# A hand-fixed order for all engines, with attention values one unit late and the causal mask on GpSimd, in a fused attention and gated-MLP kernel

## The chip, the cores and the metric

The kernel runs on one core of one Trainium2 chip. The metric is the device time of one execution in microseconds (us). Engines are named as in the profile: PE (TensorE), PEld (TensorE's weight loads), DVE (VectorE), ACT (ScalarE), POOL (GpSimd), SP (the queue that issues most DMAs).

Two states occur. Most runs of the kernel before took 436 to 441 us; one took 717.93 us, and that one was the profiled one. All comparisons below use fast runs.

## The reference, cut to what matters

The input x is 2048 x 640. It is layer-normalised, and two branches share the result. The product of both is added to x.

```python
xn = layernorm(x)                                   # 2048 x 640
# branch A: 32 heads of 20 columns, 4 segments of 512 rows
for s in range(4):
    logits = q[s] @ k[s].T * scale + causal_mask
    a_dot  = softmax(logits) @ v[s]
    a_mem  = (phi(q[s]) @ M) / (phi(q[s]) @ z + 1e-6)   # phi(t) = t+1 if t>0 else exp(t)
    o      = g * a_mem + (1 - g) * a_dot
    M += phi(k[s]).T @ v[s];  z += phi(k[s]).sum()
# branch B: sigmoid(xn @ w_gate) * (xn @ w_up) @ w_down, widths 640 -> 1536 -> 640
return x + (o @ wo) * silu(B(xn))
```

## The kernel before

Per segment there are eight groups of four heads. The scores of a group come in three units, so that the lower triangle alone is computed. Each unit's scores fill one accumulator tile `Sps` of four banks (four heads, one 32-row tile of the TensorE array each). ScalarE takes the exponential, VectorE multiplies the diagonal blocks by a mask, and TensorE then multiplies with V. All of this is in one unit, in the program's order:

```python
UNITS = [[(0, 0, 512, 0)], [(1, 0, 384, 128), (3, 384, 128, 384)], [(2, 0, 256, 256)]]
def attn_group(n, g, st_):
    for ui, unit in enumerate(UNITS):
        with prio(C0):
            for r in range(4):
                for (kb, c0, ncol, q0) in unit:
                    nc.tensor.matmul(Sps[:, r, c0:c0 + ncol], ..., tile_position=(32 * r, 0))
        nc.scalar.activation(pt[:], Sps[:, :, 0:ntot], ACT.Exp, scale=SCALE)
        for (kb, c0, ncol, q0) in unit:
            nc.vector.tensor_tensor(pt[:, :, c0:c0 + P], ..., cmask..., op=ALU.mult)
        ... # 8 or 16 matmuls of 21 columns each into Aps, then its eviction
```

Wk and Wq are loaded into a temporary tile and reordered by ScalarE (`nc.scalar.copy`, four times). The gate and up weights are loaded again for each segment. The order of the instructions of each engine is found by the framework's scheduler from priorities. Three accumulator banks, `ps_d`, serve everything but the attention.

Of the kernel before, what the change touches and what calls it, by code (L numbers as in the profile page):

```python
# [7 lines left out]
P = 128  # L9
S = 2048  # L10
D = 640
H = 32
DH = 20
NSEG = 4
# [4 lines left out]
TT = S // P  # L19
NG = 8  # L20
EPS = 1e-5
SCALE = DH ** (-0.5)

# [4 lines left out]
AX = mybir.AxisListType  # L28
PSUM = bass.MemoryType.PSUM

PAIRS = [(0, 0), (1, 0), (2, 0), (2, 1), (3, 1), (4, 1)]
PAIRS_OF_BANK = {0: [0, 1, 2], 1: [3, 4, 5]}
# [3 lines left out]
def kernel(  # L36
# [13 lines left out]
    dbg: bass.AP = None,  # L50
):
    nc = tc.nc

    PRIO_STRIDE = 1_000_000
    C0, CA, CB, CC = 0, 1, 2, 3
    prio_cnt = {}

    class prio:
        def __init__(self, cls):
            self.cls = cls  # L60

        def __enter__(self):
            self.saved = tc.cur_priority
            tc.cur_priority = self.cls * PRIO_STRIDE + prio_cnt.get(self.cls, 0)

        def __exit__(self, *a):
            prio_cnt[self.cls] = tc.cur_priority - self.cls * PRIO_STRIDE
            tc.cur_priority = self.saved
            return False

# [8 lines left out]
    stg = ctx.enter_context(tc.tile_pool(name="stg", bufs=2))  # L79
# [4 lines left out]
    wpool = ctx.enter_context(tc.tile_pool(name="wpool", bufs=2))  # L84
    xpool = ctx.enter_context(tc.tile_pool(name="xpool", bufs=2))

    dpool = ctx.enter_context(tc.tile_pool(name="dscratch", bufs=1, space=bass.MemoryType.DRAM))
    Qs = [dpool.tile([2 * 336, L], BF, name=f"Qs{i}") for i in range(2)]
    Ks = [dpool.tile([D, L], BF, name=f"Ks{i}") for i in range(2)]

    ident = cpool.tile([P, P], BF, name="ident")
    nc.gpsimd.memset(ident[:], 0.0)
    nc.gpsimd.affine_select(out=ident[:], in_=ident[:], compare_op=ALU.not_equal, fill=1.0,
                            base=0, pattern=[[-1, P]], channel_multiplier=1)

    cmask = cpool.tile([P, P], BF, name="cmask")
    nc.gpsimd.memset(cmask[:], 1.0)
    nc.gpsimd.affine_select(out=cmask[:], in_=cmask[:], compare_op=ALU.is_ge, fill=0.0,
                            base=0, pattern=[[1, P]], channel_multiplier=-1)
# [5 lines left out]
    Wd = cpool.tile([P, FC, D], BF, name="Wd")  # L105


    with prio(CC):
        beta_b = cpool.tile([P, H], BF, name="beta_b")
        nc.sync.dma_start(beta_b[:], A_beta.partition_broadcast(P))  # L110
        th = cpool.tile([P, H], F32, name="th")
        nc.scalar.activation(th[:], beta_b[:], ACT.Tanh, scale=0.5)
        gcol = cpool.tile([P, H], F32, name="gcol")
        omg = cpool.tile([P, H], F32, name="omg")
        ginv = cpool.tile([P, H], F32, name="ginv")
        nc.vector.tensor_scalar(gcol[:], th[:], 0.5, 0.5, op0=ALU.mult, op1=ALU.add)
        nc.vector.tensor_scalar(omg[:], th[:], -0.5, 0.5, op0=ALU.mult, op1=ALU.add)
        nc.vector.reciprocal(ginv[:], gcol[:])
        ginv_s = cpool.tile([P, H], F32, name="ginv_s")
        nc.vector.tensor_copy(ginv_s[:].rearrange("p (a r g) -> p a r g", a=2, r=4),  # L120
                              ginv[:].rearrange("p (a g r) -> p a r g", a=2, g=4))

        epst = cpool.tile([P, 1], F32, name="epst")
        nc.vector.memset(epst[:], EPS)

        B16 = cpool.tile([P, 16], F32, name="B16")
        nc.gpsimd.memset(B16[:], 0.0)
        for t in range(8):
            nc.gpsimd.affine_select(out=B16[:], in_=B16[:], compare_op=ALU.not_equal, fill=1.0,
                                    base=-16 * t, pattern=[[-1, 16]], channel_multiplier=1)  # L130
        Ind = cpool.tile([P, DC, H], F32, name="Ind")
        nc.gpsimd.memset(Ind[:], 0.0)
        for c in range(DC):
            if c < 2:
                nc.gpsimd.tensor_copy(Ind[:, c, 0:16], B16[:])
            elif c > 2:
                nc.gpsimd.tensor_copy(Ind[:, c, 16:32], B16[:])
            else:
                nc.gpsimd.tensor_copy(Ind[0:64, c, 0:16], B16[0:64, :])
                nc.gpsimd.tensor_copy(Ind[64:128, c, 16:32], B16[64:128, :])  # L140

        BD = cpool.tile([P, len(PAIRS), 16, DH + 1], BF, name="BD")
        nc.gpsimd.memset(BD[:], 0.0)
        for pi, (c, b) in enumerate(PAIRS):
            if c != 2:
                nc.gpsimd.tensor_copy(BD[:, pi], B16[:].unsqueeze(2).to_broadcast([P, 16, DH + 1]))
            else:
                lo, hi = (0, 64) if b == 0 else (64, 128)
                nc.gpsimd.tensor_copy(BD[lo:hi, pi], B16[lo:hi, :].unsqueeze(2).to_broadcast([hi - lo, 16, DH + 1]))

        Mbd = cpool.tile([P, len(PAIRS), 16 * (DH + 1)], BF, name="Mbd")

        QTp = cpool.tile([P, NG, L], BF, name="QTp")
        KTp = cpool.tile([P, NG, L], BF, name="KTp")
        nc.gpsimd.memset(QTp[:], 0.0)
        nc.gpsimd.memset(KTp[:], 1.0)


    Sps = ps_s.tile([P, 4, L], F32, name="Sps")

    xnT_of = {}

    def layernorm_chunk(n):
        xnT = xpool.tile([P, DC, L], BF, name="xnT")
        xnT_of[n] = xnT
        xt4 = lnp.tile([P, 4, D], BF, name="xt4")
        nc.sync.dma_start(xt4[:], x2[n * L:(n + 1) * L, :].rearrange("(j p) d -> p j d", p=P))
        mv4 = lnp.tile([P, 4, 2], F32, name="mv4")
        for j in range(4):
            st = lnp.tile([P, 2, 6], F32, name="st")  # L170
            nc.vector.bn_stats(st[:, 0, :], xt4[:, j, 0:D // 2])
            nc.vector.bn_stats(st[:, 1, :], xt4[:, j, D // 2:D])
            nc.vector.bn_aggr(mv4[:, j, :], st[:])
        sd4 = lnp.tile([P, 4], F32, name="sd4")
        nc.scalar.activation(sd4[:], mv4[:, :, 1], ACT.Sqrt, bias=epst[:], scale=1.0)
        rstd4 = lnp.tile([P, 4], F32, name="rstd4")
        nc.vector.reciprocal(rstd4[:], sd4[:])
        for j in range(4):
            xn = lnp.tile([P, D], BF, name="xn")
            nc.vector.tensor_scalar(xn[:], xt4[:, j, :], mv4[:, j, 0:1], rstd4[:, j:j + 1],  # L180
                                    op0=ALU.subtract, op1=ALU.mult)
            pT = ps_d.tile([P, DC, P], BF, name="pT", tag="d")
            for c in range(DC):
                nc.tensor.transpose(pT[:, c, :], xn[:, c * P:(c + 1) * P], ident[:])  # L184
            nc.vector.tensor_copy(xnT[:, :, j * P:(j + 1) * P], pT[:])

    seg_state = {}

    def phi_from(src, dst_pool, name, bufs):
        mn = stg.tile([P, L], BF, name="mn")  # L190
        nc.vector.tensor_scalar(mn[:], src, 0.0, None, op0=ALU.min)
        ex = stg.tile([P, L], BF, name="ex")
        nc.scalar.activation(ex[:], mn[:], ACT.Exp)
        ph = dst_pool.tile([P, L], BF, name=name, bufs=bufs)
        nc.vector.scalar_tensor_tensor(out=ph[:], in0=src, scalar=0.0, in1=ex[:], op0=ALU.max, op1=ALU.add)  # L195
        return ph

    def qkv_K(n, c, st_):
        T0 = n * L
        ps = ps_d.tile([P, L], F32, name="psk", tag="d")  # L200
        for k in range(DC):
            nc.tensor.matmul(ps[:], lhsT=Wk[:, k, c * P:(c + 1) * P], rhs=xnT_of[n][:, k, :],  # L202
                             start=(k == 0), stop=(k == DC - 1))
        if c == 0:
            st_["ktd5"] = stg.tile([P, DC, L], BF, name="ktd5", bufs=1)
        ktd = st_["ktd5"][:, c, :]
        nc.vector.tensor_copy(ktd, ps[:])
        if c == DC - 1:
            nc.sync.dma_start(Ks[n % 2].rearrange("(c p) n -> p c n", p=P), st_["ktd5"][:])
        nc.vector.tensor_reduce(out=st_["kabs"][:, c:c + 1], in_=ktd, axis=AX.X, op=ALU.max,  # L210
                                apply_absolute_value=True)
        nc.vector.tensor_scalar(st_["IK"][:, c, :], Ind[:, c, :], st_["kabs"][:, c:c + 1], -1.0,
                                op0=ALU.mult, op1=ALU.mult)
        if n < NSEG - 1:
            st_["phiKT"].append(phi_from(ktd, stg, "phikt", 5))
# [233 lines left out]
    with prio(CB):  # L449
# [11 lines left out]
        for s_ in qkv_steps(0):  # L461
            s_()
# [69 lines left out]
```

## Time and profile before

The median of four runs was 437.36 us (436.31 to 717.93). The page of the profiled run, which fell in the slow state, begins so. A line has busy us, the share of the span, and the number of instructions of each engine.

```profile
span 716.2 us, 8687 instructions
PE 670.2 (94%) x3530; PEld 282.3 (39%) x3560; DVE 284.2 (40%) x711; ACT 268.8 (38%) x290; POOL 18.2 (3%) x49
```

Read alone it says "TensorE-bound". The timeline of TensorE, below, says why that is not to be carried over to the 437 us runs. Columns are start, length, engine, line, operation, operands, count.

```profile
653.84 2.61 PE L339 MATMUL up<-xnT,wu 128*128 128x512 bf16 x5
656.17 2.61 PE L335 MATMUL gp<-xnT,wg 128*128 128x512 bf16 x5
658.50 2.61 PE L339 MATMUL up<-xnT,wu 128*128 128x512 bf16 x5
```

Groups of five matmuls of 512 columns start 2.33 us apart, 466 ns for each matmul. (The lengths shown, 2.61 us, overlap, because the profile models a matmul's end.) The Trainium skill, "TensorE: Matmul & The Clock Gate", Part 1, gives 215.7 ns for this shape on a warm array.

The groups that the argument is about, from part 5 of the same page (busy us, mean ns of one, then the idle time before them):

```profile
L388 ACT ACTIVATE pt<-Sps 128x2048 bf16<-128x2048 f32 (+1 forms) x96 | 152.9, 1593 | 136.9 <-PE Sps L383 123.9
L390 DVE TENSOR_TENSOR pt<-pt,cmask 128x512 bf16<-128x512 bf16 x128 | 51.2, 421 | 78.4 <-ACT pt L388 78.2
L383 PE MATMUL Sps<-QTp,KTp 21*128 21x128 bf16 (+3 forms) x512 | 46.7, 394 | 15.1 <-ACT pt L388 14.3
```

### The profile page before, as it was taken

The numbers are of one execution on the slowest core, as the hardware profiler recorded it, in microseconds if no ns is written. First come the engines' busy times: TensorE is split into PE (matmuls) and PEld (weight loads), VectorE is DVE, ScalarE is ACT, GpSimd is POOL, SyncE is SP. The second block draws the span as 40 slices with busy tenths as digits, with TensorE's granted clock in tenths as the row PEclk, the third lists the DMA queues.
The fourth block names the chain that finished last, engine by engine and source line by source line (L and its number), as shares of the span: only waits on it lengthen the run. The fifth ranks groups of instructions, "written<-read, shape, count | busy, mean of one in ns | idle before, by whom it ended". The sixth has DMA issues, their size and how long they took to land.

```text
span 716.2 us, 8687 instructions
## 1 busy us (share of the span) xinstructions
PE 670.2 (94%) x3530; PEld 282.3 (39%) x3560; DVE 284.2 (40%) x711; ACT 268.8 (38%) x290; POOL 18.2 (3%) x49
## 2 busy tenths in 40 slices
PE   2799999999999999996999999999699999999997
PEld 1235333334355543332335544333233554333454
DVE  4754566423323676411223457342112344511122
ACT  4632458555413543325413552022541355311111
POOL 9000000000000000000000000000000000000000
DMA  9623022112201001223120010031412001121010
GB/s 305 190 72 97 3 91 78 49 33 83 59 18 38 6 15 39 81 66 76 38 74 19 19 38 1 18 100 43 99 38 73 20 19 38 38 68 42 1 37 19
DMA packets 51432, 40.16 MB, mean 56 GB/s; under 512 B 2592, under 2 KB 50080, under 8 KB 51392
## 3 DMA queue, kind: packets, MB, share of 16 engines
q1 hardware_dynamic: 51392, 39.60, 18.9%
q8 instruction: 28, 0.46, 0.3%
q14 instruction: 12, 0.10, 0.0%
HBM read 31.60 MB, written 8.00 MB: 55 GB/s over the span
## 4 chain that ended last, share of the span: by engine, by line
PE 90%; ACT 4%; issue 3%; DVE 2%; POOL 0%; another core or an unknown queue 0%; ACTq 0%; POOLq 0%
PE yp L429 15%; PE up L339 14%; PE gp L335 14%; PE psv L257 6%; PE sp L439 6%; PE psk L202 6%; PE Sps L383 6%; PE psq L221 6%; PE Aps L396 5%; ACT pt L388 3%; PE dm L284 3%; PE am L362 3%; PE po L420 1%; PE cps L243 1%; PE pT L184 1%
## 5 line engine op out<-in xcount | busy, mean ns | idle before, releaser
L388 ACT ACTIVATE pt<-Sps 128x2048 bf16<-128x2048 f32 (+1 forms) x96 | 152.9, 1593 | 136.9 <-PE Sps L383 123.9
L339 PE MATMUL up<-xnT,wu 128*128 128x512 bf16 x229 | 121.8, 666 | 2.3 <-issue 1.6
L335 PE MATMUL gp<-xnT,wg 128*128 128x512 bf16 x229 | 120.2, 666 | 3.0 <-issue 2.5
L429 PE MATMUL yp<-Wd,hT 128*128 128x320 bf16 x384 | 117.2, 498 | 0.0
L390 DVE TENSOR_TENSOR pt<-pt,cmask 128x512 bf16<-128x512 bf16 x128 | 51.2, 421 | 78.4 <-ACT pt L388 78.2
L344 DVE SCALAR_TENSOR_TENSOR hT<-tg,up 128x512 bf16<-128x512 bf16 x48 | 32.9, 686 | 116.5 <-PE up L339 111.4
L342 ACT ACTIVATE tg<-gp 128x512 bf16<-128x512 f32 x48 | 28.5, 597 | 127.5 <-PE gp L335 125.6
L429 PEld LDWEIGHTS <-hT 128*128 128x128 bf16 x384 | 53.3, 144 | 44.0 <-issue 13.0
L383 PE MATMUL Sps<-QTp,KTp 21*128 21x128 bf16 (+3 forms) x512 | 46.7, 394 | 15.1 <-ACT pt L388 14.3
L396 PEld LDWEIGHTS <-pt 128*128 128x128 bf16 x1280 | 47.2, 102 | 30.6 <-issue 16.5
L335 PEld LDWEIGHTS <-wg 128*128 128x128 bf16 x240 | 32.9, 141 | 62.2 <-issue 60.7
L339 PEld LDWEIGHTS <-wu 128*128 128x128 bf16 x240 | 32.6, 138 | 61.5 <-issue 59.5
L396 PE MATMUL Aps<-vaug,pt 128*128 128x21 bf16 x1280 | 53.4, 178 | 0.9 <-DVE phikt L195 0.3
L221 PE MATMUL psq<-xnT,Wq 128*128 128x512 bf16 x97 | 48.0, 666 | 4.9 <-ACT Wq L457 4.0
L439 PE MATMUL sp<-Wo,oT 128*128 128x320 bf16 x160 | 51.1, 497 | 0.0
L257 PE MATMUL psv<-Wv,xnT 128*128 128x320 bf16 x160 | 49.8, 489 | 0.0
L202 PE MATMUL psk<-xnT,Wk 128*128 128x512 bf16 x95 | 47.0, 666 | 1.8 <-issue 1.2
L383 PEld LDWEIGHTS <-KTp 21*128 21x128 bf16 x512 | 11.5, 91 | 77.7 <-issue 75.8
L433 DVE SCALAR_TENSOR_TENSOR aa<-t,yp 128x320 bf16<-128x320 bf16 x32 | 15.6, 486 | 59.9 <-ACT t L432 59.9
L432 ACT ACTIVATE t<-yp 128x320 bf16<-128x320 f32 x32 | 14.0, 436 | 56.5 <-PE yp L429 56.5
L257 PEld LDWEIGHTS <-xnT 128*128 128x128 bf16 x160 | 20.5, 134 | 25.9 <-issue 15.3
L439 PEld LDWEIGHTS <-oT 128*128 128x128 bf16 x160 | 22.5, 145 | 18.9 <-issue 6.2
(82 smaller groups left out, 468.7 us busy)
## 6 DMA issues: line engine op xcount, KB each, us to landing
wg<-in_B_w_gate_dram SPq DMA_DIRECT2D x24, 320.0 KB
wu<-in_B_w_up_dram SPq DMA_DIRECT2D x24, 320.0 KB
QTp<-Qs SPq DMA_DIRECT2D x32, 84.0 KB
xt<-in_A_x_dram SPq DMA_DIRECT2D x4, 640.0 KB
Ks<-ktd SPq DMA_DIRECT2D x4, 640.0 KB
KTp<-Ks SPq DMA_DIRECT2D x32, 80.0 KB
xr<-in_A_x_dram SPq DMA_DIRECT2D x16, 160.0 KB
out_dram<-xr SPq DMA_DIRECT2D x16, 160.0 KB
```

The source lines that it names most:

```text
L202: nc.tensor.matmul(ps[:], lhsT=Wk[:, k, c * P:(c + 1) * P], rhs=xnT_of[n][:, k, :], start=(k == 0), stop=(k == DC - 1))
L221: nc.tensor.matmul(ps[:], lhsT=Wq[:, k, c * P:(c + 1) * P], rhs=xnT_of[n][:, k, :], start=(k == 0), stop=(k == DC - 1))
L257: nc.tensor.matmul(ps[:], lhsT=xnT_of[n][:, k, j * P:(j + 1) * P], rhs=Wv[:, k, half * (D // 2):(half + 1) * (D // 2)], start=(k == 0), st ...
L335: nc.tensor.matmul(gp[:], lhsT=wt["g"][:, k, fo:fo + P], rhs=xnT_of[n][:, k, :], start=(k == 0), stop=(k == DC - 1))
L339: nc.tensor.matmul(up[:], lhsT=wt["u"][:, k, fo:fo + P], rhs=xnT_of[n][:, k, :], start=(k == 0), stop=(k == DC - 1))
L344: nc.vector.scalar_tensor_tensor(out=h[:], in0=tg[:], scalar=1.0, in1=up[:], op0=ALU.add, op1=ALU.mult)
L383: nc.tensor.matmul(Sps[:, r, c0:c0 + ncol], lhsT=KTp[32 * r:32 * r + DH + 1, g, kb * P:(kb + 1) * P], rhs=QTp[32 * r:32 * r + DH + 1, g, q ...
L388: nc.scalar.activation(pt[:], Sps[:, :, 0:ntot], ACT.Exp, scale=SCALE)
L390: nc.vector.tensor_tensor(pt[:, :, c0:c0 + P], pt[:, :, c0:c0 + P], cmask[:].unsqueeze(1).to_broadcast([P, 4, P]), op=ALU.mult)
L396: nc.tensor.matmul(Aps[:, qb, r, :], lhsT=pt[:, r, off:off + P], rhs=st_["V"][kb][:, 16 * (g // 4) + 4 * r + (g % 4), :], start=first, sto ...
L429: nc.tensor.matmul(yp[:], lhsT=hT[f][:, j * P:(j + 1) * P], rhs=Wd[:, f, hs], start=(f == 0), stop=(f == FC - 1))
L439: nc.tensor.matmul(sp[:], lhsT=oT[:, c, :], rhs=Wo[:, c, hs], start=(c == 0), stop=(c == DC - 1))
```

## The change

Its intent is to leave nothing to the scheduler. Every engine's order is the program's order. A list of "A" work (next segment's normalisation, projections, memory) and a queue of "B" work (gate, up, down, output) are dealt out so that each of the 96 score units gets the same amount of TensorE work beside it. The attention values of a unit are computed one unit later, in the middle of that filler. In detail:

- the mask becomes a GpSimd `affine_select`;
- gate and up weights stay in SBUF; Wk and Wq are used in the order in which they lie in memory, and the DMA that lays K and Q out sorts the heads;
- the memory's matrices shrink from 6 blocks of 336 columns to 5 blocks of 147 or 168, block-diagonal by head;
- |q| is taken by VectorE as a bit mask, 1/sqrt by GpSimd as a power; ScalarE keeps only functions of one table;
- 14 warm-up matmuls stand at the start.

The core of the diff, cut:

```diff
-            nc.scalar.activation(pt[:], Sps[:, :, 0:ntot], ACT.Exp, scale=SCALE)
-            for (kb, c0, ncol, q0) in unit:
-                nc.vector.tensor_tensor(pt[:, :, c0:c0 + P], pt[:, :, c0:c0 + P],
-                                        cmask[:].unsqueeze(1).to_broadcast([P, 4, P]), op=ALU.mult)
+        nc.scalar.activation(pt[:, :, 0:ntot], Sps[:, :, 0:ntot], ACT.Exp, scale=SCALE)
+        for (kb, c0, ncol, q0) in unit:
+            nc.gpsimd.affine_select(out=pt[:, :, c0:c0 + P], in_=pt[:, :, c0:c0 + P], compare_op=ALU.is_ge,
+                                    fill=0.0, base=0, pattern=[[0, 4], [1, P]], channel_multiplier=-1)
 ... (cut)
         for g in range(NG):
-            with prio(CA):
-                attn_group(n, g, st_)
-            with prio(CB):
-                for s_ in step_slices[g]:
-                    s_()
 ... (cut)
+            for ui in range(NU):
+                slot = g * NU + ui
+                scores(g, UNITS[ui])
+                pt = exps(ui, UNITS[ui])
+                due += rate
+                pop(slot, due - rate / 2)      # half of this unit's filler
+                if pend is not None:
+                    attend(*pend)              # attention values of the unit before
+                pend = (n, g, ui, pt)
+                pop(slot, due)                 # the other half
```

## The prediction

> **What bounds the kernel now.** The profiled execution is not the one to beat: it took 717.93 us, the three other runs 436.3 to 438.3. In the trace TensorE is busy 94% of 716 us. The chain of waits has five back-to-back 128x512 matmuls in 2.33 us, 466 ns each, although the granted clock reads 1.000; VectorE and ScalarE durations look ordinary. The Trainium skill ("TensorE: Matmul & The Clock Gate", Part 1) gives 426.7 ns cold and 215.7 ns warm at N=512; 466 is near the cold one. I take the 436 us runs to be warm; this trace cannot show that.
>
> TensorE's warm load, estimated from the program's columns: projections, GLU, memory, transposes 660,000 columns / 2.4 = 275 us, plus about 5 us fixed cost; scores 1.36 us per group of heads in the trace, halved, x32 = 21 us; the 1280 attention-value matmuls, 27 ns each in bursts (the timeline), 35 us at either clock. Sum 335 us. So the fast run idles TensorE about 100 us: it is no longer bound by TensorE but by start-up and handoffs. Start-up: ScalarE reorders Wk and Wq (4 x 3.15 us, with 1.28 us table loads), Q is not begun before 29.5 us and the first score is at 61 us (slow clock; I estimate 47 warm). Handoffs: one score buffer, exponentials of 1.88 us, 1.88 us and 1.02 us per group, ScalarE 269 us and VectorE 284 us in all, and matmuls queued in program order.
>
> **What changes.** Removed: the weight reordering (12.6 us ScalarE), the Sqrt tables, and Abs (12.5 us on ScalarE, now on VectorE); the mask product on VectorE (51.2 us), which goes to GpSimd, where a 512-element select costs an estimated 0.55 us, 70 us in all, hidden because attention values are taken one unit later; gate and up weights loaded once, not four times (DMA is idle, worth little); memory matmuls narrowed from 48,000 to 18,000 columns (12.6 us warm). Added: cheap warm-up matmuls, and a fixed order which gives every score unit about 2.5 us of filler on TensorE, half before and half after the previous unit's attention values. Since exponential plus handoff takes about 2.2 us, the next scores should usually find their buffer free. ScalarE and VectorE work of the body falls only little: about 2.5 us and 2.6 us per unit against TensorE's 3.1.
>
> **On the critical path.** Warm TensorE load after: 335 - 12 = 323 us. Start-up: scores should begin at about 31 us, since the K and Q spills stand behind 7 MB of loads (305 GB/s in the first slice before); TensorE has some 20 us of work by then, so about 12 us are lost. Tail: 4 us. That is 339 us without a stall. In the body, in-order engines at 80% load and three shared accumulators should cost 5 to 8% of 300 us, 18 us.
>
> **Prediction: 357 us, range 341 to 380. Faster by over 2%: 0.97; within 2%: 0.02; slower: 0.01.** If the profiled execution is again slow, its span should still be 650 to 700 us, because there TensorE's load rules: the gain shows only at the warm clock.
>
> **What would show each step.** 128x512 matmuls at about 216 ns apart in a warm trace; TensorE idle under 40 us; first score near 31 us; ScalarE total 235 to 250 us; mask groups on GpSimd near 0.55 us; memory groups a third of the columns; waits of scores on exponentials small.
>
> **What would make it wrong.** GpSimd selects slowed by sharing SBUF access with VectorE, so attention values wait; phi exponentials (up to 1536 columns) ahead of a score exponential; loads delaying the spills beyond 35 us; or the clock falling in gaps.

## The result, and the profile after

The changed kernel took 387.97 us (median of 11 runs, 386.88 to 390.41), all fast. The kernel before took 438.33 us (median of its 16 runs, the four above among them). The ratio of the fast runs is 0.8858 (95% interval 0.8831 to 0.8885). Ratios here are the mean time of one kernel's fast runs over that of the other's of the same rounds, so not quite the ratio of the medians. The change is 11% faster, but 31 us slower than predicted, and above the upper end of the range.

To compare like with like I ran the kernel before again, unchanged, for a profile. Its page (span, part 1, the granted clock in 40 slices, and the chain that ended last) reads:

```profile
span 436.1 us, 8717 instructions
PE 379.9 (87%) x3560; PEld 204.4 (47%) x3560; DVE 275.1 (63%) x711; ACT 265.0 (61%) x290; POOL 18.4 (4%) x49
PEclk9968999989999999999969999899977999999999
PE 65%; DVE 17%; ACT 12%; issue 3%; DMA 1%; POOL 1%; SPq 0%; ACTq 0%; DVEq 0%; POOLq 0%
```

The same lines of the changed kernel, and its groups for the mask, the exponentials and the attention values:

```profile
span 386.5 us, 8606 instructions
PE 355.4 (92%) x3522; PEld 199.5 (52%) x3566; DVE 234.3 (61%) x526; ACT 232.9 (60%) x247; POOL 101.2 (26%) x169
PEclk9899999999999998999999998999999999999989
PE 68%; DVE 15%; ACT 8%; issue 4%; DMA 4%; POOL 0%; SPq 0%; DVEq 0%; ACTq 0%
L427 ACT ACTIVATE pt<-Sps 128x2048 bf16<-128x2048 f32 (+1 forms) x96 | 152.8, 1592 | 59.6 <-PE Sps L419 56.9
L429 POOL TENSOR_SCALAR_AFFINE_SELECT pt<-pt 128x512 bf16<-128x512 bf16 x128 | 84.2, 668 | 262.7 <-ACT pt L427 262.7
L443 PE MATMUL Aps<-V,pt 128*128 128x21 bf16 x1280 | 46.9, 173 | 0.3 <-POOL pt L429 0.3
```

Two things are to be read. The mask costs GpSimd 84 us, and GpSimd waits 262.7 us for exponentials, yet TensorE waited 0.3 us for the mask. And TensorE is shown busy for 355.4 of 386.5 us, 31 us idle, which would fit the prediction's "under 40 us". That figure deceives: a matmul is shown busy for longer than its share of the array, so gaps of 0.1 us between two matmuls vanish in it.

A better account counts starts. In the fast traces the matmuls' starts, back to back, are 216 ns apart at 512 columns, 136 at 320, 56 at 128, and 25.5 for the attention values' 21 columns. The program's matmuls at these distances, without the scores, come to 301 us in the changed kernel (its 14 warm-up matmuls not counted) and 312 us in the one before. The scores' columns come to 17 us in both, if the four row tiles run together. What is left of each span is neither. (I computed this from the starts in the trace; the few 512-column records that are missing from it are counted.)

| us | before | after | predicted for after |
|---|---|---|---|
| matmuls without scores, at full pace | 312 | 301 | 302 |
| scores, columns alone | 17 | 17 | 21 in all |
| switches into and out of score blocks (see below) | about 20 | 20 | 0 |
| lost before the first score | 29 | 13 | 12 |
| lost in the body (waits, half clock) | 54 | 24.5 | 18 |
| lost after the last attention values | 4 | 11 | 4 |
| span | 436 | 386.5 | 357 |

The switches' row is 96 times 0.21 us, which an experiment below measured; the lost time of the body is what then remains. The device time lies about 1.5 us over the span. So the change gained 11 us of TensorE work, 16 us of start-up and about 29 us in the body, and it gave 7 us back at the end. Against the prediction, 16 us went to the scores, 7 us to the end, 6.5 us to the body and 1 us to the start.

Part of the body's loss is the clock. By the clock events of the two traces TensorE had half its clock for 27 us of the body before and for 7 us of it after. At half pace that is at most 14 and 3 us of the 54 and 24.5 us.

What TensorE waited for in the kernel before, in the fast state (total us, times, longest):

```profile
PE Sps L383 <- ACT pt L388: 18.5, 14, 3.7
PE pT L184 <- POOL B L129: 12.3, 1, 12.3
PE psq L221 <- ACT Wq L457: 8.0, 2, 5.4
PE Aps L396 <- DVE pt L390: 4.9, 13, 0.9
```

The second is the wait before the first matmul of all, the third the wait for Wq, which ScalarE reorders: both belong to the start. The same view of the changed kernel, with the line that corresponds to the first of these last:

```profile
PE pk L306 <- DVE ktd L301: 5.2, 3, 2.6
PE pT L205 <- DVE xn L191: 3.4, 5, 1.2
PE po L393 <- DVE odot L387: 1.9, 1, 1.9
PE Sps L419 <- ACT pt L427: 1.1, 3, 0.4
```

Scores hardly wait for exponentials any more (1.1 us against 18.5). Waits at the segment boundaries are new at the top: `pk` is the transposition of phi(K), once per boundary.

The trace shows three places to look at. First, a block of scores in the timeline (the PEld row is its weight load):

```profile
329.63 0.84 PE L407 MATMUL sp<-Wo,oT 128*128 128x320 bf16 x5
330.40 0.10 PEld L419 LDWEIGHTS <-KT 21*128 21x128 bf16 x4 [0.26 <-issue]
330.40 0.40 PE L419 MATMUL Sps<-QT,KT 21*128 21x512 bf16 x4
330.73 1.04 PE L353 MATMUL gp<-xnT,Wg 128*128 128x512 bf16 x4
```

Five matmuls of 320 columns should take 0.68 us at 136 ns; the block starts 0.77 us after them. The block's four matmuls run side by side, 512 columns, 0.214 us; the next matmul starts 0.33 us later. So about 0.09 us is lost ahead of the block and 0.12 us after it. The weights of the small tile are loaded only at 330.40, when the large matmuls are through.

Second, a segment boundary:

```profile
142.82 0.34 PE L306 MATMUL pk<-ident,ktd 128*128 128x128 bf16 x3
143.16 0.88 DVE L182 BATCH_NORM_STATS2 st<-xt 128x6 f32<-128x320 bf16 x2
144.20 0.64 DVE L301 TENSOR_TENSOR ktd<-ktd,mn 128x1024 bf16<-128x1024 bf16 x1
144.89 0.84 PE L306 MATMUL pk<-ident,ktd 128*128 128x128 bf16 x12 [1.72 <-DVE ktd L301]
```

TensorE needs the last piece of phi(K), the addition at 144.20. In front of it in VectorE's queue stands a statistic of the next segment's normalisation, which nobody needs soon. TensorE waits 1.72 us, and soon after the granted clock is halved for 3.4 us (the 8 in the 16th slice of the clock row).

Third, the end, where the last residual rows are loaded into a buffer that is still being stored:

```profile
377.99 0.33 SPq L399 DMA_DIRECT2D xr<-in_A_x_dram  x1
380.31 0.49 DVE L413 TENSOR_TENSOR xr<-aa,xr 128x640 bf16<-128x640 bf16 x1 [1.39 <-DMA xr<-in_A_x_dram]
380.70 0.33 SPq L399 DMA_DIRECT2D xr<-in_A_x_dram  x1
383.04 0.49 DVE L413 TENSOR_TENSOR xr<-aa,xr 128x640 bf16<-128x640 bf16 x1 [1.44 <-issue]
```

### The profile page after: what moved, and what is told of

It is laid out like the page before. It is cut to its first block, busy times and chain, and to the rows that moved or that the text cites. A ratio compares the mean times of both kernels' runs of the same rounds, so it can differ in the third digit from the quotient of the medians.

```text
span 386.5 us, 8606 instructions
## 1 busy us (share of the span) xinstructions
PE 355.4 (92%) x3522; PEld 199.5 (52%) x3566; DVE 234.3 (61%) x526; ACT 232.9 (60%) x247; POOL 101.2 (26%) x169
## 4 chain that ended last, share of the span: by engine, by line
PE 68%; DVE 15%; ACT 8%; issue 4%; DMA 4%; POOL 0%; SPq 0%; DVEq 0%; ACTq 0%
PE psq L222 11%; PE yp L376 11%; PE up L362 10%; PE gp L353 10%; PE Aps L443 6%; PE Sps L419 5%; ACT pt L427 4%; PE sp L407 4%; PE psv L280 4%; DVE hT L365 3%; DVE st L182 2%; DMA xt<-in_A_x_dram 2%; PE cps L266 1%; PE pk L306 1%; ACT mn L295 1%
## 5 line engine op out<-in xcount | busy, mean ns | idle before, releaser
L429 POOL TENSOR_SCALAR_AFFINE_SELECT pt<-pt 128x512 bf16<-128x512 bf16 x128 | 84.2, 668 | 262.7 <-ACT pt L427 262.7
L362 PE MATMUL up<-xnT,Wu 128*128 128x512 bf16 x224 | 59.8, 383 | 1.5 <-DVE omem L346 0.4
L353 PE MATMUL gp<-xnT,Wg 128*128 128x512 bf16 x223 | 58.1, 379 | 2.9 <-ACT oT L395 1.7
L376 PE MATMUL yp<-Wd,hT 128*128 128x320 bf16 x384 | 57.5, 299 | 0.1
L443 PE MATMUL Aps<-V,pt 128*128 128x21 bf16 x1280 | 46.9, 173 | 0.3 <-POOL pt L429 0.3
L419 PE MATMUL Sps<-QT,KT 21*128 21x128 bf16 (+3 forms) x512 | 35.6, 303 | 2.3 <-ACT pt L427 1.1
L407 PE MATMUL sp<-Wo,oT 128*128 128x320 bf16 x160 | 28.5, 318 | 1.3 <-ACT V L285 1.1
L280 PE MATMUL psv<-Wv,xnT 128*128 128x320 bf16 x160 | 26.5, 311 | 0.0
L222 PE MATMUL psq<-xnT,Wk 128*128 128x512 bf16 x93 | 23.7, 379 | 2.0 <-DVE xnT L210 1.5
L222 PE MATMUL psq<-xnT,Wq 128*128 128x512 bf16 x96 | 24.1, 380 | 0.2
```

The costliest lines, as they stand in the source:

```text
L222: nc.tensor.matmul(ps[:], lhsT=W[:, k, c * P:(c + 1) * P], rhs=xnT_of[n][:, k, :], start=(k == 0), stop=(k == DC - 1))
L280: nc.tensor.matmul(ps[:], lhsT=xnT_of[n][:, k, j * P:(j + 1) * P], rhs=Wv[:, k, half * HD:(half + 1) * HD], start=(k == 0), stop=(k == DC ...
L353: nc.tensor.matmul(gp[:], lhsT=Wg[:, k, f * P:(f + 1) * P], rhs=xnT_of[n][:, k, :], start=(k == 0), stop=(k == DC - 1))
L362: nc.tensor.matmul(up[:], lhsT=Wu[:, k, f * P:(f + 1) * P], rhs=xnT_of[n][:, k, :], start=(k == 0), stop=(k == DC - 1))
L376: nc.tensor.matmul(yp[:], lhsT=s["hT"][f][:, j * P:(j + 1) * P], rhs=Wd[:, f, hs], start=(f == 0), stop=(f == FC - 1))
L407: nc.tensor.matmul(sp[:], lhsT=s["po"][j][:, c, :], rhs=Wo[:, c, hs], start=(c == 0), stop=(c == DC - 1))
```

## The experiments

Theory A is the prediction's own arithmetic. Theory B is that what it missed is (1) a switch cost on each score block, (2) the order of VectorE's and ScalarE's queues at the segment boundaries, and (3) a chain at the end. Rivals are named in each expectation. "After" is 387.97 us, ratio 0.8858. Every run gave correct results. Times are medians; the ratios are to the kernel before in the same rounds.

### The kernel before, again

No edit.

> The kernel before, unchanged, for a profile in the fast state; wanted: about 437 us, five 128x512 matmuls in about 1.08 us instead of 2.33. Theory A (the prediction's arithmetic): TensorE's own work is about 335 us of it and a block of scores costs TensorE about 0.22 us on average. Theory B (a block of scores also costs a switch on each side that does not shrink with the clock): about 0.40 us per block with the switch before it, and TensorE's own work is about 350 us. Either way 80 to 100 us of TensorE idle, more than the 52 us over the ideal pitch that the changed kernel shows.

It took 437.94 us, and gave the fast profile above. Outside TensorE's own work there were 87 us in the table's count, in the expected range. About half of the blocks of scores (48 of 95) take the same 0.33 or 0.22 us there as in the changed kernel, and the others longer, so B's cost is not something that the change brought in.

### Attention values in the same unit

```diff
-                if pend is not None:
-                    attend(*pend)
-                pend = (n, g, ui, pt)
                 pop(slot, due)
+                attend(n, g, ui, pt)
 ... (cut: the last `attend(*pend)` goes too)
```

> The changed kernel with each unit's attention values taken at the end of the same unit instead of one unit later, all else kept. If the one-unit delay is what the change gains by, TensorE waits for the exponential and the select at the end of each unit: 1.88 + 0.67 us and handoffs, about 2.9 us, against 2.5 us of filler, so 0.4 to 0.9 us for most of 96 units: 425 to 470 us, as slow as the kernel before. If the fixed filler alone carries the gain: under 400 us.

It took 428.15 us (ratio 0.9785). Undoing this one step takes back 40 of the 50 us. The largest wait of TensorE is now the mask, which had cost it 0.3 us:

```profile
PE Aps L443 <- POOL pt L429: 31.4, 56, 1.4
```

So the fixed filler alone is not enough; the one-unit delay is what hides exponential and mask. No run puts the delay alone into the kernel before, so what the hand-fixed order gives by itself is not shown.

### The mask on VectorE, and on GpSimd in the kernel before

```diff
-            nc.gpsimd.affine_select(out=pt[:, :, c0:c0 + P], ...)
+            nc.vector.tensor_tensor(pt[:, :, c0:c0 + P], ..., cmask..., op=ALU.mult)
 ... (cut: `cmask` is made at the start)
```

> The changed kernel with the causal mask back on VectorE as a product (128 times about 0.42 us, 51 us more VectorE work), as before the change. If moving the mask to GpSimd is a part of the gain: 5 to 20 us slower than 388, with longer waits of TensorE at the segment boundaries. Rival (VectorE has room and the mask is off the path): within 3 us of 388.

It took 460.19 us (ratio 1.0511): slower than the kernel before. I had expected 5 to 20 us and got 72 us. The reason is in VectorE's waits:

```profile
DVE pt L434 <- ACT pt L432: 106.8, 78, 4.0
```

VectorE was busy 60% of the span (61% in the changed kernel), but it stood 106.8 us in front of a mask whose exponential was not done. The Trainium skill ("TensorE: Matmul & The Clock Gate", the table at its head) calls the queues of ScalarE, VectorE and GpSimd strict FIFOs. This trace agrees: the evictions behind the mask waited too. Here a memory product `am` ends at 356.30, but its eviction into `rm` starts only at 358.46, behind a mask for which VectorE had stood idle 1.62 us:

```profile
355.96 0.34 PE L343 MATMUL am<-Mbd,qtd 128*128 128x147 bf16 x3
358.11 0.42 DVE L434 TENSOR_TENSOR pt<-pt,cmask 128x512 bf16<-128x512 bf16 x1 [1.62 <-ACT pt L432]
358.46 0.17 DVE L348 SCALAR_TENSOR_TENSOR rm<-am,ginv 128x16 f32<-128x16 f32 x1
```

The clock fell as well. The body has 48 us at half clock, against 7 us in the changed kernel; at half pace that is up to 20 of the 72 us. The opposite edit in the kernel before tests whether the move alone is the gain:

```diff
-                nc.vector.tensor_tensor(pt[:, :, c0:c0 + P], ..., cmask..., op=ALU.mult)
+                nc.gpsimd.affine_select(out=pt[:, :, c0:c0 + P], ...)
```

> The kernel before with one part of the change: the mask as a GpSimd select instead of a VectorE product. If VectorE's load is what binds the kernel before: 5 to 12 us less than 438. If its handoff chain binds (scores, exponential, mask, attention values in the same unit): no gain, 0 to 8 us slower, since the select takes 0.67 us against 0.42 us.

It took 442.8 us (ratio 1.0088, interval 1.0041 to 1.0136): no gain, a little slower, within the 2% that counts as the same. VectorE had 41 us less to do and it bought nothing there. VectorE's load was not what bound the kernel before.

### The mask on VectorE, queued one unit later

```diff
+                if pend is not None:
+                    mask(*pend[2:])        # of the unit before, its exponential is done
                 scores(g, UNITS[ui])
 ... (cut: `mask`, the product of the run above, taken out of `exps`)
```

> The changed kernel with the mask on VectorE, as in the run that took 460 us, but queued there one unit later, in front of the next unit's scores, when its exponential is done. VectorE has the same 51 us more to do in both. If the 72 us came from the order (VectorE stands in front of each mask until the exponential ends, and every eviction behind it waits): most of it goes, 388 to 405. If they came from VectorE's load: 440 or more.

It took 410.39 us (ratio 0.9378), a little above the expected 388 to 405. The masks' idle time is gone:

```profile
L437 DVE TENSOR_TENSOR pt<-pt,cmask 128x512 bf16<-128x512 bf16 x128 | 50.8, 418 | 0.0
```

With the same VectorE work, 50 of the 72 us went away by the order alone, and with them most of the half clock (3 us of it in this body). The remaining 22 us are what the mask costs VectorE when it is queued well; TensorE waited 15.9 us in it for masks. So the gain from GpSimd is mostly that it has nothing else to do: its waits hold up nobody.

### The scores twice

```diff
+        for _ in range(2):
             for r in range(4):
                 for (kb, c0, ncol, q0) in unit:
                     nc.tensor.matmul(Sps[:, r, c0:c0 + ncol], ...)
```

> The changed kernel with every block of scores computed twice in a row into the same accumulators (result unchanged). Theory A (the prediction's 0.22 us per block): 96 more blocks add 19 to 22 us. Theory B (inside a block, from its first matmul to the next instruction's, the trace has 0.34, 0.33 and 0.22 us for the three units, 29 us in all, because loading four small tiles is not hidden): 26 to 32 us more, 414 to 420. If TensorE has slack in the body: under 15 us.

It took 398.86 us (ratio 0.9103): 11 us more, below both theories' numbers. The timeline tells why:

```profile
331.06 0.61 PE L420 MATMUL Sps<-QT,KT 21*128 21x512 bf16 x8
331.60 0.58 PE L407 MATMUL sp<-Wo,oT 128*128 128x320 bf16 x3
```

The doubled block takes 0.54 us instead of 0.33: the repeat costs 0.21 us, its columns alone. All blocks together grew by 16 us inside. So the columns cost 17 us in the whole kernel, and whatever else a block costs is paid once per block, not per matmul. Of 16 us more TensorE work, 11 us showed in the time, so about a third disappears in waits.

### A tiny block, to measure the switch by itself

```diff
+    def tiny(g):
+        nc.tensor.matmul(aps_of["t"][:, 352:368], lhsT=KT[0:E1, g, 0:P], rhs=QT[0:E1, g, 0:16],
+                         start=False, stop=True, tile_position=(0, 0), skip_group_check=True)
 ... (in the second and third unit of a group, before the attention values; its result is never read)
```

> The changed kernel with one extra matmul in 64 of the 96 units, of one 32-row tile as the scores use and of 16 columns only (7 ns of columns at the warm clock), between the filler and the attention values; its result is never read. It measures the switch to a small row tile and back by itself. Switch theory: about 0.1 us before it and about 0.1 us after it, 10 to 14 us more TensorE work in all, of which at least half shows in the time: 393 to 402. If small tiles switch freely: under 0.05 us each, within 2 us of 388.

It took 395.23 us (ratio 0.9025): 7 us more. The timeline of one:

```profile
333.05 0.71 PE L407 MATMUL sp<-Wo,oT 128*128 128x320 bf16 x4
333.69 0.18 PE L461 MATMUL Aps<-QT,KT 21*128 21x16 bf16 x1
333.80 0.56 PE L444 MATMUL Aps<-V,pt 128*128 128x21 bf16 x16
```

Four matmuls of 136 ns end after 0.54 us, and the small tile starts after 0.64 us; the next matmul starts 0.11 us after it, though it has only 16 columns. Over the 63 recorded ones the medians are 96 ns ahead and 110 ns after, together 0.21 us, 13 us in all. The switch cost is shown by itself. It fits what the Trainium skill says in "TensorEngine Tiling (Array Packing)", Key Properties: "Changing tiling mode (not just tile) drains the TensorE". 96 score blocks pay about 20 us. The time grew by 7 of the added 13 us, so by the same measure the 16 us by which the scores were mis-sized explain some 9 to 11 us of the 31 us (an estimate from these two runs).

### The statistics behind phi(K)

```diff
             for part in range(2):
                 it.append((0, 2250, lambda part=part: phi(n, "kt", "phik", part)))
-                it.append((0, 1100, lambda part=part: stats(2 * part)))
-                it.append((0, 1100, lambda part=part: stats(2 * part + 1)))
+                it.append((0, 1100, lambda part=part: stats(part)))
                 it.append((0, 830, lambda part=part: phi_end(n, "phik", part)))
+            for j in (2, 3):
+                it.append((0, 1100, lambda j=j: stats(j)))
```

> The changed kernel with two of the four layer-norm statistics of the next segment moved on VectorE from in front of the end of phi(K) to behind it. Theory B (VectorE's order at the three segment boundaries holds TensorE up, and the clock then halves for 3.4 us): the wait of the phi(K) transposes (5.2 us on VectorE's ktd, 1.5 us on hT) falls under 2 us, the half-clock stretches at 146 and 232 us go, and the time falls by 5 to 9 us, to 379 to 383. Rival (VectorE's total load is what counts there, its order only shifts the wait): within 2 us of 388.

It took 383.83 us (ratio 0.876): 4 us less, just short of the expected 5 to 9. The wait of `pk` on `ktd` left the list of TensorE's waits, and the half-clock stretch at 146 us is gone. The one of the next segment stayed (at 224 us in this run, 232 in "after"): there ScalarE had taken up phi's exponential before VectorE had made its input, stood 3.06 us in front of it, and the score exponential and an accumulator's eviction waited behind it; TensorE waited 3.30 us for that eviction:

```profile
222.26 1.06 ACT L295 ACTIVATE mn<-mn 128x1024 bf16<-128x1024 bf16 x1 [3.06 <-DVE mn L294]
223.96 2.16 PE L362 MATMUL up<-xnT,Wu 128*128 128x512 bf16 x5 [3.30 <-ACT oT L395]
```

So part (2) holds, with ScalarE's queue as well as VectorE's; but at 222 us the order only moved the wait, as the rival said.

### The last residual rows from SBUF

```diff
+        if n == NSEG - 1:
+            s["xr", j] = xt_of[n][:, j, :]
+            return
         xr = fpool.tile([P, D], BF, name="xr", bufs=2)
 ... (cut)
```

> The changed kernel with the residual rows of the last segment taken from the copy of x that is still in SBUF, instead of loaded again into two rotating buffers. Theory B (the last 6.7 us after the last matmul are a chain of buffer, load and store): 2 to 4 us less, 384 to 386. Rival (the end is bound by the last output matmuls and the last store alone): under 1 us.

It took 385.61 us (ratio 0.8803): 2.4 us less, as B expected. In the profiles the loss after the last attention values fell from 10.9 to 8.3 us (9.8 to 10.9 in those that leave the end as it is). The rest is the last attention eviction, the sum, transposition and output product in a row. The version meant to beat both, below, also splits the sum, and its profile has 6.6 us there; the split was not tested alone.

### One warm-up matmul instead of fourteen

```diff
-    WARM = 14
+    WARM = 1
```

> The changed kernel with 1 warm-up matmul instead of 14. The prediction called them cheap. If they warm the clock for the first transposes and values: 1 to 4 us slower, with more half-clock time before 30 us. If the trace is right that the half-clock stretch at 9.7 us comes anyway, and loads set the start: within 1 us.

It took 389.05 us (ratio 0.8884, interval 0.8853 to 0.8915, against 0.8831 to 0.8885 for after). The first score moved from 33.3 to 34.7 us in the profiles (31.6 to 33.3 us in all that keep the fourteen). About 1 us, at the edge of what the runs resolve.

### A version meant to beat both

From "after": the last rows from SBUF as above, and phi(K) taken apart. Its minimum (VectorE), its exponential (ScalarE) and its addition (VectorE) are dealt out with memory products between them, the statistics come last, and the sum of both attention parts is made two row blocks at a time.

```diff
+            for part in range(2):
+                it.append((0, 1250, lambda part=part: phi_min(n, "kt", "phik", part)))
+                take(1)                    # one memory product (a statistic in segment 0)
+                it.append((0, 1000, lambda part=part: phi_exp(n, "phik", part)))
+                take(2 if n else 1)
+                it.append((0, 830, lambda part=part: phi_end(n, "phik", part)))
+            it += fill + st4               # what is left of them, then the statistics
```

(The last line stands for two; the other parts of the edit are cut.)

> A version meant to beat both: the last segment's x from SBUF, the phi(K) steps spread between the memory products so that neither VectorE nor ScalarE waits in order for the other, statistics after them, the sum of the two attention parts two row blocks at a time. Theory B: the waits at the three boundaries and most of the half-clock stretches go: 374 to 380 us. Rival (VectorE's and ScalarE's total work at the boundaries counts, not its order): 380 to 384, no more than the two single edits give together.

It took 378.44 us (377.09 to 381.56; ratio 0.8648, interval 0.8609 to 0.8686), 2.4% less than the changed kernel and the fastest kernel here. Both single edits together would give about 381.5 us; the other 3 us are from spreading phi(K) and splitting the sum, which were not tested apart. By the count of the table the body lost 18.6 us in its profile (24.5 in "after") and the end 6.6 (10.9). Its page:

```profile
span 376.2 us, 8596 instructions
PE 350.9 (93%) x3522; PEld 197.3 (52%) x3566; DVE 233.3 (62%) x526; ACT 232.3 (62%) x247; POOL 101.0 (27%) x169
PEclk9899999999999999999999999999999999999999
```

Between start and end the clock is not halved any more. The engines do the same work as in "after"; only its order differs.

### Fewer score blocks

The 256-column units of two neighbouring groups share one block: 80 blocks instead of 96.

```diff
+PAIR = [
+    [(0, 0, 0, 512, 0)],
+    [(0, 1, 0, 384, 128), (0, 3, 384, 128, 384)],
+    [(0, 2, 0, 256, 256), (1, 2, 256, 256, 256)],
+    [(1, 0, 0, 512, 0)],
+    [(1, 1, 0, 384, 128), (1, 3, 384, 128, 384)],
+]
 ... (cut)
```

> The 378 us version with the 256-column units of two neighbouring groups in one block, so 80 score blocks instead of 96, the same columns. If a block costs TensorE about 0.21 us beside its columns (0.095 us before it, 0.115 us after): 3.4 us less TensorE work and 2.7 us less ScalarE work, 374 to 376. If that cost is hidden: within 1 us of 378.4.

It took 391.33 us (ratio 0.8938), 13 us slower than the version it was made from: a miss. Its largest TensorE wait tells of a cost that I had left out:

```profile
PE Aps L465 <- DVE odot L478: 6.8, 8, 2.0
```

The joint unit ends one group's attention accumulator and opens the next one's, and there is only one such accumulator; TensorE waits for VectorE to empty it. The waits at the boundaries were longer too, perhaps because all the filler fell elsewhere. So this run neither confirms nor refutes the saving by fewer switches.

## Why the prediction was wrong

- **"I take the 436 us runs to be warm."** Right: the pitch (the distance of starts) of 512-column matmuls is 216 ns in the fast traces. But that 466 ns lies near the skill's cold figure was a coincidence, a mean of 443 and 556, and "this trace cannot show that" overlooked the 128-column starts 56 ns apart in the same trace. The guess at the idle TensorE time of the kernel before ("about 100 us") was near: 107 us if the switches count as idle, 87 if not.
- **"Scores 1.36 us per group of heads in the trace, halved, x32 = 21 us."** This is the first failed step. The measured term is 37 us: 17 us of columns and 20 us of switches. Halving took the slow trace for the same work at half the clock, which it was not: a unit's block, from its first start to the next instruction's, takes 0.44, 0.45 and 0.22 us in it (medians of the three units) and 0.33, 0.34 and 0.22 us in the changed kernel. The shortest does not shrink at all. The 0.1 us ahead of each block was not in the term either. The page on tiling told of the drain; the prediction did not use it. In the table this step is 16 of the 29.5 us; by the runs that added TensorE work, it explains about a third of the 31 us of time.
- **"In-order engines at 80% load and three shared accumulators should cost 5 to 8% of 300 us, 18 us."** Somewhat small: 24.5 us, which is the 8%. But the loss was not spread over the units, as a percentage suggests. About 13 us of it are gaps of over 0.25 us at the three segment boundaries (near 50, 145 and 235 us), where a queued instruction with an unready input blocks everything behind it. Reordering, with no work removed, took back 4 us and, done with the last rows from SBUF and the split sum, 9.5 us.
- **"Tail: 4 us."** The second failed step: 11 us. It had no chain of buffer, load and store in it, and no serial sum. 2.4 us was the chain of two residual buffers, shown; the rest is a serial end, of which splitting the sum took perhaps 1.7 us (8.3 to 6.6 in two profiles, not tested alone).
- **Start-up.** First score predicted at 31 us, measured 33.3; lost time 12 against 13. Right.
- **"A 512-element select costs an estimated 0.55 us, 70 us in all, hidden."** 0.67 us and 84 us, and hidden: 0.3 us of TensorE waiting. (The estimate can be had from the trace before, where selects of 16 and 128 elements take 0.22 and 0.29 us: in a straight line, 0.54 us at 512.) The reason that it matters was not in the prediction. It saw 51 us taken from VectorE; the runs show that the order is the larger part (50 of 72 us).
- **ScalarE 235 to 250 us:** 232.9, slightly below. **Waits of scores on exponentials small:** 1.1 us, right.
- **"TensorE idle under 40 us"** was met as the page counts (31 us), while the time was missed. It was a bad test, because busy time hides the 0.1 us gaps.
- **Of the named dangers,** "phi exponentials ahead of a score exponential" did occur, but in the run with the statistics moved (3.06 us at 222 us; in the changed kernel itself ScalarE waited at most 1.2 us for such an input); the clock did fall in gaps, for 3.4 us at a time; loads did not delay the first score beyond 35 us (33.3).

What stays open: why the kernel before has a slow state, in which long matmuls start 466 ns apart on average at a granted clock shown as 1.000; how much of the 20 us of switches can be avoided; what the hand-fixed order gives without the delay, and the delay without it; and the rest of the end.

## What to carry to other kernels

When work is queued in program order on in-order engines, look not only at how long an instruction takes but at how long it stands in front of the others with its input unready; put such an instruction on an engine with nothing else to do, or queue it one unit later. Before scaling a measured term with the clock, take apart what scales (columns) and what is paid per block (switches between tile shapes), check in the trace's short matmuls that it is the clock that differs, and judge TensorE by the distance of starts, not by busy time. At stage boundaries and at the end, check buffer counts and queue order by hand: here they gave 9.5 us at no cost in work.

## What the Trainium skill lacked or had wrong

- "TensorEngine Tiling (Array Packing)", Key Properties, says that a change of tiling mode drains the array but gives no figure, and "TensorE: Matmul & The Clock Gate", Part 3, gives the distance of starts within a pack (about 4 ns; 3 to 4 ns here for the one-matmul-per-tile units) and a tail for semaphores, but no cost of going from the full array to small tiles. The runs show 96 ns before and 110 ns after a small block between full-array matmuls, 0.21 us for going and coming back.
- "TensorE: Matmul & The Clock Gate", the table of "Why this matters for your kernels", warns of idle gaps over about 3 us. Here shorter ones came before a half clock: near 230 us TensorE waited 1.51 and then 2.57 us within 4.5 us, and the clock was halved for 3.4 us from the end of the second; near 143 us it waited 1.55 and 1.72 us, and the half clock began 1.3 us later. Where moving the statistics took the 1.72 us away, that stretch went too.
- The same page, Part 1, gives 426.7 ns cold and 215.7 ns warm for 512 columns. The traces agree: 216 ns in the fast ones, 427 ns for the first warm-up matmuls of the changed kernel. The page cautions that clock events of a trace can be unreliable, but no page that I read has the slow state of the kernel before: 512-column matmuls 443 or 556 ns apart, part of the 128-column ones 56 ns apart, at a granted clock of 1.000 for the whole of 716 us.
